# A spectral mixing layer and its MLP: GpSimd's groups and the filter copy moved forward in the first batch, the second batch's evacuations shared by two engines

## The chip, the cores and the metric

One core of a Trainium2 chip runs the whole kernel. The metric is device time in microseconds (us), from launch to end. "Span" is a little less: the time from the first to the last instruction in a profiled execution. Runs of one kernel differ here by about 2 us. Times are therefore compared over several runs, and traces stage by stage. All runs below are fast ones. Engines: ACT is ScalarE, DVE is VectorE.

## The reference

```python
# x (8, 3008, 256), filt_r and filt_i (1505, 256), all fp32
X = np.fft.rfft(x, axis=1)
y = np.fft.irfft(X * (filt_r + 1j * filt_i)[None], n=3008, axis=1)
h = y.reshape(24064, 256) @ w_in            # w_in (256, 2048)
out = np.maximum(0.01 * h, h) @ w_out       # w_out (2048, 256)
```

## The kernel before

The transform of 3008 points is split as 94 x 32. Per batch: matmuls over 94 (`s1`), evacuation (a copy out of PSUM, where matmuls leave their results) to fp16, 32x32 transposes on DVE (`t1`), matmuls over 32 (`s2`), the filter product, matmuls back (`sa`), evacuation, transposes (`t2`), matmuls (`sb`). The MLP runs in slots of one hidden-layer group each; the transform of the next batch is interleaved into these slots. The first batch has nothing to hide behind, so it has code of its own, in two halves of 128 channels, where some filter products go to DVE straight from PSUM, and some to GpSimd by way of a copy by ACT.

```python
outp = ctx.enter_context(tc.tile_pool(name="outst", bufs=4))
php = ctx.enter_context(tc.tile_pool(name="php", bufs=2, space=bass.MemoryType.PSUM))
pfp = ctx.enter_context(tc.tile_pool(name="pfp", bufs=3, space=bass.MemoryType.PSUM))
...
def s1_group(b, g):                      # two matmuls into one PSUM buffer, one evacuation
    def go():
        ps = pfp.tile([P, 2, D], FP32, tag="pf", ...)
        ...
        spread(big[(4 * b) % 3], 2 * g, ps, nc.scalar.copy)      # L174
    return go
...
def first_s2(hf, c, n, on_pool):
    ps = php.tile([P, n, DH], FP32, tag="ph", ...)
    for j in range(0, n, 4):
        nc.tensor.matmul(...)                                     # L253
    if on_pool:
        y = [outp.tile([P, n, DH], FP16, tag="ost", ...) for i in range(2)]
        for j, xf in enumerate(xs):
            act(xf[:], ps[:, ts(j, 4), :])                        # L261
        ... nc.gpsimd.tensor_tensor(y[i]..., AL.mult)             # L264
    else:
        y = [ypp.tile([P, n, DH], FP16, tag=f"yw{i}", bufs=2, ...) for i in range(2)]
        for i in range(2):
            nc.vector.tensor_tensor(y[i][:], ps[:], fs[i], AL.mult)   # L269
def first_sa(hf, c): ...                 # reads y (L277), evacuated by ACT (L174)
def upper(hf): ...                       # filter copied to partitions 64-127: fa by ACT, fb by DVE (L282)
...
plan(1, 0, 0, 3, 6, 10, 4, 3, 25, 31)    # batch 1: s1 from slot 0, three a slot; t1 at 6, s2 at 10, t2 at 25, sb at 31
for slot in range(SL * (NCHUNK + 1)):
    ci, g = divmod(slot, SL)
    if ci < NCHUNK: moe1_group(ci, g)    # 4 matmuls (L339), leaky ReLU by ACT (L344)
    for f in tasks.get(slot, ()): f()
    if ci > 0: moe2_slice(ci - 1, g)     # 8 matmuls (L353)
```

Cuts are marked by dots. `t1` is L186, `t2` L194, the later batches' `s1` L163, `s2` L203, `sb` L230.

Of the kernel before, what the change touches and what calls it, by code (L numbers as in the profile page):

```python
# [65 lines left out]
def kernel(  # L66
# [9 lines left out]
    nc = tc.nc  # L76
# [25 lines left out]
    big = [cpool.tile([P, Q * D], FP16, name=f"big{i}") for i in range(3)]  # L102
# [19 lines left out]
    def x_load(b, n0=0, nn=N2, d0=0, dn=D):  # L122

        for lo, cnt in ((0, R1),) if b + 1 < B else ((0, 64), (64, N1 - 64)):
            nc.gpsimd.dma_start(  # L125
                x_sb[lo : lo + cnt, ds(n0, nn), ds(d0, dn)],
                bass.AP(tensor=x.tensor, offset=x.offset + (b * N + lo * N2 + n0) * D + d0,
                        ap=[[N2 * D, cnt], [D, nn], [1, dn]]))
# [10 lines left out]
    step = N2 // FP  # L139
# [15 lines left out]
    nc.vector.memset(big[2][:].rearrange("p (e n t) -> p e n t", n=Q, t=2)[:, :, NC:Q, :], 0.0)  # L155


    def s1_group(b, g):
        def go():
            ps = pfp.tile([P, 2, D], FP32, tag="pf", name=f"s1_b{b}_g{g}")  # L160
            for j in range(2):
                n2 = 2 * g + j
                nc.tensor.matmul(ps[:, j, :], f1_sb[:N1, n2, :], x_sb[:N1, n2, :],  # L163
                                 start=True, stop=True)
            spread(big[(4 * b) % 3], 2 * g, ps, nc.scalar.copy)
        return go


    def paired(t):
        return t[:].rearrange("p (e n t) -> p n e t", n=Q, t=2)  # L170

    def spread(dst, n0, ps, copy, e0=0):
        nn, de = ps.shape[1], ps.shape[2] // 2
        copy(paired(dst)[:, ds(n0, nn), ds(e0, de)], ps[:].rearrange("p n (e t) -> p n e t", t=2))  # L174
# [3 lines left out]
    def t1_part(b, i, flat=False):  # L178
        def go():
            a = big[(4 * b) % 3][:].bitcast(FP32)[:, ts(i, E4 * Q)].rearrange("p (e n) -> p e n", n=Q)  # L180
            o = big[(4 * b + 1) % 3][:].bitcast(FP32)
            if flat:
                o = o[:, ts(i, E4 * Q)].rearrange("p (e n) -> p e n", n=Q)
            else:
                o = o.rearrange("p (n e) -> p e n", n=Q)[:, ts(i, E4), :]
            nc.vector.transpose(o, a)  # L186
        return go


    def t2_part(b, i):  # L190
        def go():
            a = big[(4 * b + 2) % 3][:].bitcast(FP32)[:, ts(i, E4 * Q)].rearrange("p (e n) -> p e n", n=Q)
            o = big[(4 * b + 3) % 3][:].bitcast(FP32).rearrange("p (h n e) -> p h e n", h=2, n=Q)
            nc.vector.transpose(o[:, i // 2, ts(i % 2, E4), :], a)  # L194
        return go
# [3 lines left out]
    def s2_group(b, g):  # L199
        def go():  # L200
            ps = pfp.tile([P, 2, D], FP32, tag="pf", name=f"s2_b{b}_g{g}")
            src = big[(4 * b + 1) % 3][:].rearrange("p (n d) -> p n d", n=Q)
            nc.tensor.matmul(ps[:], fwd2, src[:, ds(2 * g, 2), :], start=True, stop=True)  # L203
            fa, fb = fa_sb[:, ds(2 * g, 2), :], fb_sb[:, ds(2 * g, 2), :]
            p1 = scrp.tile([P, 2, D], FP32, tag="p1", name=f"p1_b{b}_g{g}")
            p2 = scrp.tile([P, 2, D], FP32, tag="p2", name=f"p2_b{b}_g{g}")
            nc.vector.tensor_tensor(p1[:], ps[:], fa, AL.mult)  # L207
            nc.vector.tensor_tensor(p2[0:64], ps[64:P], fb[64:P], AL.mult)  # L208
            nc.vector.tensor_tensor(p2[64:P], ps[0:64], fb[0:64], AL.mult)  # L209
            y1 = ypp.tile([P, 2, D], FP16, tag="y", name=f"y_b{b}_g{g}")  # L210
            nc.gpsimd.tensor_tensor(y1[:], p1[:], p2[:], AL.add)  # L211
            ys[(b, g)] = y1
        return go

    def sa_group(b, g):
        def go():
            ps = pfp.tile([P, 2, D], FP32, tag="pf", name=f"sa_b{b}_g{g}")
            nc.tensor.matmul(ps[:], inv2, ys.pop((b, g))[:], start=True, stop=True)  # L218
            spread(big[(4 * b + 2) % 3], 2 * g, ps, nc.scalar.copy)
        return go  # L220

    def sb_group(b, g, copy, pool=(pfp, "pf")):
        dt, h = g // 8, g % 8

        def go():
            src = big[(4 * b + 3) % 3][:].rearrange("p (h n d) -> p h n d", h=2, n=Q)
            ps = pool[0].tile([P, 4, N1], FP32, tag=pool[1], name=f"sb_b{b}_g{g}")
            for j in range(4):
                n2 = 4 * h + j
                nc.tensor.matmul(ps[:, j, :], src[:, dt, n2, :], i1_sb[:, n2, :],  # L230
                                 start=True, stop=True)
            yv = yts[b % 2][:, dt, :].rearrange("p (a c) -> p a c", c=N2)
            copy(yv[:, :, ds(4 * h, 4)], ps[:].rearrange("p c a -> p a c"))  # L233
        return go
# [3 lines left out]
    act, dve = nc.scalar.copy, nc.vector.tensor_copy  # L238
# [10 lines left out]
    def first_s2(hf, c, n, on_pool):  # L249
        ps = php.tile([P, n, DH], FP32, tag="ph", name=f"f2_h{hf}_c{c}")  # L250
        src = paired(big[1])
        for j in range(0, n, 4):
            nc.tensor.matmul(ps[:, ds(j, 4), :].rearrange("p n (e t) -> p n e t", t=2), fwd2,  # L253
                             src[:, ds(c + j, 4), ts(hf, DH // 2)], start=True, stop=True)
        fs = [f[:, ds(c, n), ts(hf, DH)] for f in (fa_sb, fb_sb)]
        if on_pool:
            y = [outp.tile([P, n, DH], FP16, tag="ost", name=f"fy{i}_h{hf}_c{c}") for i in range(2)]
            xs = [scrp.tile([P, 4, DH], FP32, tag=f"p{j // 4 + 1}", name=f"fx_h{hf}_c{c + j}")
                  for j in range(0, n, 4)]
# [4 lines that stand above are left out]
                    nc.gpsimd.tensor_tensor(y[i][:, ts(j, 4), :], xf[:], fs[i][:, ts(j, 4), :], AL.mult)  # L264
        else:
            y = [ypp.tile([P, n, DH], FP16, tag=f"yw{i}", bufs=2, name=f"fy{i}_h{hf}_c{c}")
                 for i in range(2)]
            for i in range(2):
                nc.vector.tensor_tensor(y[i][:], ps[:], fs[i], AL.mult)  # L269
        ys[(hf, c)] = y  # L270

    def first_sa(hf, c):
        y = ys.pop((hf, c))
        for j in range(0, y[0].shape[1], 4):
            ps = pfp.tile([P, 4, DH], FP32, tag="pf", name=f"fa_h{hf}_c{c + j}")
            for i, m in enumerate((inv2, inv2x)):
                nc.tensor.matmul(ps[:], m, y[i][:, ds(j, 4), :], start=(i == 0), stop=(i == 1))  # L277
            spread(big[2], c + j, ps, act, hf * DH // 2)

    def upper(hf):  # L280
        for t, cp in ((fa_sb, act), (fb_sb, dve)):
            cp(t[64:P, :, ts(hf, DH)], t[0:64, :, ts(hf, DH)])  # L282
# [9 lines left out]
        first_s1(0, g, two[(g // 2) % 2], (act, dve)[g % 2])  # L292
    t1_part(0, 0, True)(), t1_part(0, 1, True)()
    upper(0)
    first_s2(0, 0, 8, False)
    first_s2(0, 8, 8, True)
    first_s2(0, 16, 4, False)
    first_s2(0, 20, 4, True)
    for g in range(8):
        first_s1(1, g, two[0], dve if g in (1, 3, 6) else act)  # L300
    x_load(1)
    t1_part(0, 2, True)(), t1_part(0, 3, True)()
    first_sa(0, 0), first_sa(0, 16)
    upper(1)
    first_s2(1, 0, 8, False)
    first_s2(1, 8, 8, True)
    nc.gpsimd.dma_start(w_out_sb[:], moe_w_out.rearrange("(ct p) d -> p ct d", p=P))
    first_sa(0, 8), first_sa(0, 20)
    first_s2(1, 16, 8, False)
    first_sa(1, 0)  # L310
    t2_part(0, 0)(), t2_part(0, 1)()
    first_sa(1, 16), first_sa(1, 8)
# [57 lines left out]
    def at(slot, f):  # L370
        tasks.setdefault(slot, []).append(f)

    def plan(b, s1, first, per, t1, s2, step, lag, t2, sb):
        for i, g in enumerate(range(first, 16)):
            at(s1 + i // per, s1_group(b, g))
        if b + 1 < B:
            at(s1 + (15 - first) // per, lambda: x_load(b + 1))
        for i in range(4):
            at(t1 + i, t1_part(b, i))
            at(t2 + i, t2_part(b, i))  # L380
        for g in range(12):
            at(s2 + (step * g) // 4, s2_group(b, g))
            at(s2 + lag + (step * g) // 4, sa_group(b, g))
        for g in range(16):
            at(sb + g // 2, sb_group(b, g, nc.vector.tensor_copy))

    plan(1, 0, 0, 3, 6, 10, 4, 3, 25, 31)
    for b in range(2, B):
        z = 47 * (b - 1) - 8
        plan(b, z, 0, 2, z + 9, z + 13, 5, 3, z + 32, z + 37)  # L390

    for slot in range(SL * (NCHUNK + 1)):
        ci, g = divmod(slot, SL)
# [36 lines left out]
```

## Time and profile before

| | before |
|---|---|
| time, 6 runs | median 793.71 us, 792.79 to 795.1 |
| profiled execution | 792.51 us, span 790.6 us |
| first batch: 17th matmul of `s1` to first MLP matmul | 11.59 to 44.73 = 33.14 us |
| first to ninth MLP group | 44.73 to 60.44 = 15.71 us |
| ninth MLP group to end | 730.20 us |

The lower three rows are differences of start times in the trace. The first stage is counted from the 17th matmul because that one waits for the input's second transfer, whose landing differs from run to run. The prediction shows the profile's lines and reads them.

### The profile page before, as it was taken

Reading aid. Unit: us, or ns where it says so; the run is one execution under the profiler, and the core shown is the slowest. Engines: PE = TensorE matmul, PEld = TensorE weight load, DVE = VectorE, ACT = ScalarE, POOL = GpSimd, SP = SyncE. Lnnn points to the kernel's source line nnn. Section 1 sums busy time; section 2 is a strip of 40 time slices with the busy share of each in tenths; the row PEclk is TensorE's granted clock in tenths of the full one; section 3 lists DMA queues with packets and bytes.
Section 4 is the critical chain, followed back from the end, with each engine's and each line's share of the span. In section 5 each row is a group of like instructions: output and inputs, shape, how many; then the busy total and the mean of one; then the engine's idle time right before and its main releaser. Section 6 shows DMA issues by size and latency. Waiting matters only on the chain.

```text
span 790.6 us, 13456 instructions
## 1 busy us (share of the span) xinstructions
PE 761.7 (96%) x5748; PEld 526.2 (67%) x5748; DVE 362.5 (46%) x451; ACT 560.3 (71%) x802; POOL 150.6 (19%) x122
## 2 busy tenths in 40 slices
PE   2788999999999999999999999999999999999998
PEld 1345667666776667866678667776677666776666
DVE  4829751675407742376415763077431765200000
ACT  3696768777596766877677776877759776666664
POOL 5863400151002500043000420024000340000000
PEclk9999999999999999999999999999999999999999
DMA  9933101410114010410105010141100101001111
GB/s 175 220 44 86 40 28 41 108 41 27 42 41 107 28 41 28 94 54 34 35 29 119 27 41 34 35 106 41 41 27 28 41 27 41 35 34 41 41 41 54
DMA packets 42011, 43.38 MB, mean 55 GB/s; under 512 B 14274, under 2 KB 40514, under 8 KB 41282
## 3 DMA queue, kind: packets, MB, share of 16 engines
q0 software_dynamic: 15760, 16.99, 13.2%
q1 hardware_dynamic: 26192, 25.53, 9.3%
q8 instruction: 45, 0.74, 0.4%
q14 instruction: 14, 0.11, 0.0%
HBM read 34.10 MB, written 24.64 MB: 74 GB/s over the span
## 4 chain that ended last, share of the span: by engine, by line
PE 92%; ACT 3%; DVE 3%; DMA 1%; issue 0%; POOL 0%; ACTq 0%; DVEq 0%; POOLq 0%
PE po_ps L353 40%; PE h_c_g L339 40%; PE sb_b_g L230 3%; PE s_b_g L163 3%; PE s_b_g L203 2%; PE sa_b_g L218 2%; ACT big L174 2%; DVE big L186 1%; DMA x_sb<-in_x_dram 1%; DVE big L194 1%; PE o_c_t L353 1%; ACT gt_c L344 1%; DVE fy_h_c L269 1%; PE f_h_g L244 1%; PE f_h_c L253 1%
## 5 line engine op out<-in xcount | busy, mean ns | idle before, releaser
L344 ACT ACTIVATE gt_c<-h_c_g 128x1024 f16<-128x1024 f32 x376 | 385.6, 1026 | 196.3 <-PE h_c_g L339 195.3
L339 PE MATMUL h_c_g<-yt,w_in_sb 128*128 128x512 f16 (+7 forms) x1728 | 386.7, 351 | 1.3 <-ACT gt_c L344 1.0
L353 PE MATMUL po_ps<-w_out_sb,gt_c 128*128 128x256 f16 x2944 | 381.4, 272 | 0.5 <-ACT ost_c_t L360 0.5
L353 PEld LDWEIGHTS <-gt_c 128*128 128x128 f16 x3008 | 290.7, 98 | 88.7 <-issue 3.8
L339 PEld LDWEIGHTS <-w_in_sb 128*128 128x128 f16 x1728 | 163.0, 98 | 96.2 <-issue 2.3
L211 POOL TENSOR_TENSOR y_b_g<-p_b_g,p_b_g 128x512 f16<-128x512 f32 x84 | 106.9, 1273 | 225.0 <-DVE p_b_g L209 225.0
L186 DVE STREAM_TRANSPOSE big<-big 128x1024 f32<-128x1024 f32 x32 | 55.7, 1844 | 141.6 <-ACT big L174 141.5
L233 DVE CAST yt<-sb_b_g 128x376 f16<-128x376 f32 x116 | 58.3, 545 | 89.9 <-PE sb_b_g L230 89.9
L207 DVE TENSOR_TENSOR p_b_g<-s_b_g,fa_sb 128x512 f32<-128x512 f32 x84 | 58.1, 692 | 37.3 <-PE s_b_g L203 34.8
L360 ACT COPY ost_c_t<-po_ps 128x256 f32<-128x256 f32 x184 | 69.4, 377 | 7.1 <-PE po_ps L353 5.9
L194 DVE STREAM_TRANSPOSE big<-big 128x1024 f32<-128x1024 f32 x32 | 58.4, 1940 | 34.2 <-ACT big L174 34.2
L174 ACT CAST big<-s_b_g 128x512 f16<-128x512 f32 x112 | 61.5, 621 | 0.0
L208 DVE TENSOR_TENSOR p_b_g<-s_b_g,fb_sb 64x512 f32<-64x512 f32 x84 | 58.2, 693 | 1.1
L125 POOL DMA_DIRECT2D x_sb<-in_x_dram x12 | 8.5, 713 | 263.0 <-PE s_b_g L163 262.2
L209 DVE TENSOR_TENSOR p_b_g<-s_b_g,fb_sb 64x512 f32<-64x512 f32 x84 | 57.4, 684 | 1.1
L174 ACT CAST big<-sa_b_g 128x512 f16<-128x512 f32 x84 | 50.6, 602 | 0.0
L230 PEld LDWEIGHTS <-big 128*128 128x128 f16 x512 | 28.7, 98 | 16.6 <-DVE big L194 2.5
L163 PE MATMUL s_b_g<-x_sb,f_sb 94*128 94x256 f16 x224 | 34.6, 272 | 1.6 <-ACT big L174 0.7
L230 PE MATMUL sb_b_g<-i_sb,big 128*128 128x94 f16 x512 | 32.5, 206 | 2.0 <-DVE big L194 1.5
L203 PE MATMUL s_b_g<-big,small_sb 128*128 128x512 f16 x84 | 31.8, 379 | 1.8 <-DVE big L186 1.8
L218 PE MATMUL sa_b_g<-y_b_g,small_sb 128*128 128x512 f16 x84 | 31.8, 379 | 0.0
L163 PEld LDWEIGHTS <-f_sb 94*128 94x128 f16 x224 | 20.9, 97 | 12.2 <-issue 4.4
(37 smaller groups left out, 135.5 us busy)
## 6 DMA issues: line engine op xcount, KB each, us to landing
out_dram<-ost_c_t SPq DMA_DIRECT2D x92, 256.0 KB, 2.1
x_sb<-in_x_dram POOLq DMA_DIRECT2D x6, 1536.0 KB, 10.8
x_sb<-in_x_dram POOLq DMA_DIRECT2D x4, 384.0 KB, 10.4
w_in_sb<-in_moe_w_in_dram POOLq DMA_DIRECT2D x1, 1024.0 KB, 15.3
w_out_sb<-in_moe_w_out_dram POOLq DMA_DIRECT2D x1, 1024.0 KB, 10.7
x_sb<-in_x_dram POOLq DMA_DIRECT2D x1, 1024.0 KB, 8.0
f_sb<-fwd_const SPq DMA_DIRECT2D x4, 192.0 KB, 3.5
fa_sb<-in_filt_r_dram POOLq DMA_DIRECT2D x4, 192.0 KB, 10.0
```

The source lines that it names most:

```text
L163: nc.tensor.matmul(ps[:, j, :], f1_sb[:N1, n2, :], x_sb[:N1, n2, :], start=True, stop=True)
L174: copy(paired(dst)[:, ds(n0, nn), ds(e0, de)], ps[:].rearrange("p n (e t) -> p n e t", t=2))
L186: nc.vector.transpose(o, a)
L194: nc.vector.transpose(o[:, i // 2, ts(i % 2, E4), :], a)
L208: nc.vector.tensor_tensor(p2[0:64], ps[64:P], fb[64:P], AL.mult)
L211: nc.gpsimd.tensor_tensor(y1[:], p1[:], p2[:], AL.add)
L230: nc.tensor.matmul(ps[:, j, :], src[:, dt, n2, :], i1_sb[:, n2, :], start=True, stop=True)
L233: copy(yv[:, :, ds(4 * h, 4)], ps[:].rearrange("p c a -> p a c"))
L339: nc.tensor.matmul(ph[:, j, ds(o, ln)], w_in_sb[:, dt, ts(ct, P)], yts[b % 2][:, dt, ds(lo, ln)], start=(dt == 0), stop=(dt == NDT - 1),)
L344: nc.scalar.activation(gts[ci][:, ds(2 * g, 2), :], ph[:], AF.Lrelu)
L353: nc.tensor.matmul(po, gts[ci][:, ct, ts(tj, P)], w_out_sb[:, ct, :], start=(ct == 0), stop=(ct == NCT - 1))
L360: nc.scalar.copy(ost[:, tj % 2, :], po)
```

## The change

Intent: bring the slower GpSimd products of the first batch forward, and take ACT's long filter copy (2.75 us) off the way of DVE; in the second batch, let the idle DVE take half of the evacuations that ACT is late with, and put the step that follows two slots later, when its data are there.

```diff
-    def s1_group(b, g):
+    def s1_group(b, g, copy=nc.scalar.copy):
...
-            spread(big[(4 * b) % 3], 2 * g, ps, nc.scalar.copy)
+            spread(big[(4 * b) % 3], 2 * g, ps, copy)
...
     upper(0)
+    first_s2(0, 8, 8, True)
     first_s2(0, 0, 8, False)
-    first_s2(0, 8, 8, True)
+    first_s2(0, 20, 4, True)
     first_s2(0, 16, 4, False)
-    first_s2(0, 20, 4, True)
...
+    upper(1)
     first_sa(0, 0), first_sa(0, 16)
-    upper(1)
-    first_s2(1, 0, 8, False)
     first_s2(1, 8, 8, True)
...
+    first_s2(1, 0, 8, False)
+    first_s2(1, 16, 8, False)
     first_sa(0, 8), first_sa(0, 20)
-    first_s2(1, 16, 8, False)
...
-            at(s1 + i // per, s1_group(b, g))
+            at(s1 + g // per, s1_group(b, g, dve if b == 1 and g % 2 else act))
...
-    plan(1, 0, 0, 3, 6, 10, 4, 3, 25, 31)
+    plan(1, 0, 3, 6, 12, 4, 3, 26, 31)
```

Left out are lines that rename things or reorder the plan. One of these matters: the loop that queues the second transposes now stands behind the one of the filter steps, because in the second batch the last `sa` and the first of these transposes now meet in slot 26. For the later batches the order of instructions stays the same.

More of the change, by code (lines that the diff above doesn't have):

```diff
@@ L371, in at, with plan @@
         tasks.setdefault(slot, []).append(f)
-    def plan(b, s1, first, per, t1, s2, step, lag, t2, sb):
-        for i, g in enumerate(range(first, 16)):
-            at(s1 + i // per, s1_group(b, g))
+    def plan(b, s1, per, t1, s2, step, lag, t2, sb):
+        for g in range(16):
+            at(s1 + g // per, s1_group(b, g, dve if b == 1 and g % 2 else act))
         if b + 1 < B:
-            at(s1 + (15 - first) // per, lambda: x_load(b + 1))
+            at(s1 + 15 // per, lambda: x_load(b + 1))
         for i in range(4):
             at(t1 + i, t1_part(b, i))
-            at(t2 + i, t2_part(b, i))
         for g in range(12):
@@ L383, in plan @@
             at(s2 + lag + (step * g) // 4, sa_group(b, g))
+        for i in range(4):
+            at(t2 + i, t2_part(b, i))
         for g in range(16):
-            at(sb + g // 2, sb_group(b, g, nc.vector.tensor_copy))
-    plan(1, 0, 0, 3, 6, 10, 4, 3, 25, 31)
+            at(sb + g // 2, sb_group(b, g, dve))
+    plan(1, 0, 3, 6, 12, 4, 3, 26, 31)
     for b in range(2, B):
         z = 47 * (b - 1) - 8
-        plan(b, z, 0, 2, z + 9, z + 13, 5, 3, z + 32, z + 37)
+        plan(b, z, 2, z + 9, z + 13, 5, 3, z + 32, z + 37)
     for slot in range(SL * (NCHUNK + 1)):
```

## The prediction

> **What bounds the kernel now.** I read the page's table of engines first, then busy times by stage, then the chain of waits through the first 67 us, then timelines of single engines there.
>
> ```profile
> PE 761.7 (96%) x5748; PEld 526.2 (67%) x5748; DVE 362.5 (46%) x451; ACT 560.3 (71%) x802; POOL 150.6 (19%) x122
> ```
>
> TensorE is busy for 761.7 of 790.6 us, so at most 28.9 us can be had from reordering. The table by stage says where they lie (start:end, length, busy us and instructions of PE, PEld, DVE, ACT, POOL, then the granted clock, DMA share and GB/s):
>
> ```profile
> 16.80:24.35 7.55, 6.27 (x38) 3.70 (x39) 6.59 (x8) 3.89 (x8) 5.31 (x6) 1.00 1.70 221
> 24.35:35.30 10.95, 6.92 (x24) 2.18 (x24) 8.35 (x9) 8.57 (x12) 7.58 (x8) 1.00 1.06 230
> 35.30:44.70 9.40, 7.21 (x79) 4.38 (x79) 8.79 (x8) 6.97 (x16) 9.32 (x2) 1.00 1.02 146
> 44.70:59.00 14.30, 11.95 (x60) 5.78 (x60) 0.40 (x1) 13.01 (x22) 7.46 (x2) 1.00 0.01 2
> 59.00:66.80 7.80, 5.54 (x33) 3.15 (x33) 7.23 (x4) 5.65 (x7) 0.00 (x0) 1.00 1.03 200
> 66.80:760.00 693.20, 692.65 (x5279) 483.65 (x5279) 324.88 (x416) 500.25 (x710) 110.08 (x90) 1.00 0.16 46
> ```
>
> From 66.8 us on TensorE is full: 692.65 of 693.2. Work there is only carried forward, so the time saved is the amount by which TensorE reaches that full state earlier, for the same work done. Before it lie two stretches that the change touches: the first batch (to 44.7) and the slots in which the second batch's first transform runs between the first MLP groups (44.7 to 66.8). The chain of waits (start, length, what) for the second:
>
> ```profile
> 46.91 1.58 ACT big L174 x3
> 48.50 0.92 ACT gt_c L344
> 49.41 1.47 ACT big L174 x3
> 50.88 0.93 ACT gt_c L344
> ...
> 58.98 0.49 ACT big L174
> 59.47 0.02 issue
> 59.49 7.24 DVE big L186 x4
> 66.73 0.04 issue
> 66.78 0.38 PE s_b_g L203
> ```
>
> ACT alone sets these slots: one leaky ReLU (0.92) and three evacuations (0.49 each), 2.39 us a slot. Then four DVE transposes follow end to end, and the PE timeline shows TensorE standing still for them:
>
> ```profile
> 63.91 1.03 PE L339 MATMUL h_c_g<-yt,w_in_sb 128*128 128x512 f16 x4
> 66.78 0.38 PE L203 MATMUL s_b_g<-big,small_sb 128*128 128x512 f16 x1 [1.84 <-DVE big L186]
> ```
>
> The same chain in the first batch, where the filter copy (L282) is on the path:
>
> ```profile
> 26.62 2.76 ACT fa_sb L282
> 29.38 0.02 issue
> 29.41 2.37 DVE fy_h_c L269 x2
> 31.77 0.05 issue
> 31.82 1.04 PE f_h_c L253 x2
> 32.85 0.02 issue
> 32.88 2.36 DVE fy_h_c L269 x2
> 35.23 7.28 DVE big L194 x4
> ```
>
> [...] the same evacuation shape (128x512 to f16) takes 0.69 us on DVE and 0.60 on ACT in the first batch. [...] GpSimd runs one 15.74 us negation from 35.82 to 51.56, over the moved evacuations. [...] DVE's casts out of PSUM at 43.11 to 45.09, under that negation, take 540 to 550 ns, and 545 is the mean of all 116. [...] here 128-column matmuls are 0.107 us apart up to about 23 us and 0.054 soon after.
>
> **The change, part by part.**
>
> (a) Slots 0 to 5: eight of 16 evacuations go from ACT to DVE, which is idle there (14.40 us before its transposes). ACT loses 8 x 0.48 = 3.85 us. ACT per pair of slots: 2 x 0.92 + 3 x 0.48 = 3.28; TensorE per pair: two MLP groups of 0.865 and six transform steps of 0.215 = 3.02; DVE 3 x 0.69 = 2.07. So ACT stays the bound, narrowly, at 1.64 a slot, and the queue of three PSUM buffers adds small waits. I stepped through the slots with the program's own buffer order (in the built program, group 3 reuses the buffer of 1, 4 of 0, 5 of 2, 6 of 3, 7 of 5, ...), intervals from the trace, 0.38 us from a step's issue to its end, 0.69 for DVE. MLP group 8 then issues at 56.50 where the trace of before has 60.44: 3.94 us gained.
>
> (b) The transposes start when the last evacuation ends: about 55.1 instead of 59.49, so they end at 62.35. The transform that needs them is also moved, from slot 10 to 12. From group 8 on a slot takes 0.865 + 0.87 = 1.735 us, so slot 12 starts at 56.50 + 4 x 1.735 = 63.44 and its first filter matmul would issue at 64.30, two us after the transposes. The wait disappears: from the issue end of the last MLP matmul (63.91 + 4 x 0.217 = 64.78) to 66.78 that is 2.00 us (the 1.84 of the timeline counts a modelled end). As TensorE has no gap later, moving the matmuls to a later slot costs nothing by itself.
>
> (c) Second transposes one slot later (26), their users still from slot 31. Before, the first starts 2.67 us after slot 24 begins (97.86 less 95.19) and four take 7.30. After: slot 26 + 2.67 + 7.30 = + 9.97; the first user is at + 9.75 (0.865 + 0.215 + 0.87 + 4 x 1.735 + 0.865) but needs only the first two transposes, done at about + 6.4. No stall.
>
> (d) First batch, first half. GpSimd's groups now come first through TensorE, so DVE's first filter product waits for the fourth matmul: 18.73 instead of 17.96. Its two products then end at 21.08, not 20.31. In the built program groups 20 and 16 now share one PSUM buffer, so 16 also waits for ACT's copy of 20: matmul at 20.24, ready at 20.83, hidden behind DVE. DVE reaches the next evacuation at 22.37 instead of 21.84, + 0.5. TensorE's group 4 waits for that buffer and group 7 in turn for group 4's, so the transposes start at about 25.4 instead of 24.92.
>
> (e) First batch, second half. The filter copy starts when ACT's last evacuation is done, 25.4, ends at 28.15 instead of 29.37, and leaves the path. But DVE's group is now second in TensorE: transposes end 27.29 + 0.49 = 27.78, the fourth matmul 1.93 later, so the product starts at about 29.75 against 29.41. Had (d) cost nothing, (e) would have gained only 0.15. From there the same steps follow (2.37, 1.09, 2.36, transposes): + 0.34 us at the start of the MLP. The evacuations pushed behind the copy end at about 35.2, just before the transposes need them at 35.5.
>
> Sum: - 3.94 - 2.00 + 0.34 = - 5.6 us. Nothing else moves: later batches have the same instructions in the same order.
>
> **The rivals.**
> 1. The reordering of the first batch pays as intended: the 1.13 us that DVE waits for the filter copy goes. For it: that wait is on the chain. Against: the copy's removal exposes TensorE's fourth matmul 0.15 us later. Time 786.3.
> 2. Buffers bind rather than ACT in slots 0 to 5: for it, three PSUM buffers and TensorE at 3.02 per 3.28; a chain matmul, evacuation, matmul costs about 1.1 us a group. If half of (a) is lost, 789.8.
> 3. The moved evacuations are slowed by GpSimd's negation. Only those before 51.56 can be, about four; doubled, that costs up to 2 us: 789.8. The 540 to 550 ns above speak against it.
> 4. The compressed distance between second transposes and their users stalls TensorE at slot 31. Were the dependency on all four transposes, 9.97 against 9.75 plus latency would cost some 0.3 us.
> 5. The gain is hidden, since TensorE is 96% busy: 793. Against it: the chain of waits has the slots' ACT work and the transposes on it, and TensorE never waits later for anything that could absorb them.
>
> **Range and chances.** 793.4 - 5.6 = 787.8 us. The first batch is uncertain by about a microsecond either way ([...]tight buffers), the slots by about 0.7, and the three runs of before spread over 2.3. Range 786.0 to 789.6. A change of 2% would be 15.9 us, more than half of all idle time of TensorE and three times my sum; nothing lengthens the full stretch. Faster by over 2%: 0.01; within: 0.98; slower: 0.01.
>
> **What would show it.** (a) ACT's leaky ReLUs in slots 0 to 5 come alternately about 1.9 and 1.4 us apart; eight DVE casts of 128x512 at about 0.69 us. (b) No wait of the filter matmul (L203) for the transposes (L186). (c) No wait of L230 for L194 after 100 us. (d), (e) The DVE product L269 of the second half waits for TensorE, not for the copy L282, and starts near 29.75; the first MLP matmul at about 45.1. Full state at the second batch's first filter matmul: about 64.6. The prediction is wrong if the MLP starts before 44.5 or after 45.8, if a slot still takes over 1.9 us on average, or if TensorE's idle time does not fall by about 5 to 6 us.

## The result, and the profile after

The changed kernel took 788.21 us (median of 6 runs, 787.49 to 789.27), before in the same rounds and earlier 793.71. The ratio is 0.9931, interval 0.9918 to 0.9944. The output is correct. Predicted were 787.8 us and a range from 786.0 to 789.6.

The page's engine line of the changed kernel: TensorE has the same 5748 matmuls, in a span that is 3.9 us shorter.

```profile
PE 762.2 (97%) x5748; PEld 527.3 (67%) x5748; DVE 367.9 (47%) x459; ACT 557.1 (71%) x794; POOL 150.6 (19%) x122
```

The stages of the changed kernel, with the same columns as in the prediction (stretch, length, busy us and instructions of PE, PEld, DVE, ACT, POOL, then clock, DMA share, GB/s):

```profile
25.00:36.00 11.00, 8.02 (x21) 2.47 (x20) 8.41 (x8) 7.18 (x10) 2.03 (x3) 0.84 1.08 237
46.60:58.46 11.86, 11.12 (x64) 6.18 (x64) 7.23 (x10) 10.57 (x15) 10.51 (x2) 1.00 0.27 37
58.46:66.30 7.84, 7.84 (x53) 5.08 (x52) 6.00 (x4) 5.55 (x7) 0.00 (x0) 1.00 0.82 173
66.30:756.00 689.70, 689.15 (x5256) 481.34 (x5255) 324.71 (x416) 499.18 (x708) 110.07 (x90) 1.00 0.16 46
```

The slots that took 14.30 us for 11.95 us of TensorE's work now leave it 0.74 us idle in 11.86, and from 58.46 on TensorE is full; before it was from 66.8. The first line is a warning: the mean clock is 0.84 there, and GpSimd worked only 2.03 us in that stretch, against 7.58 in the one of before. (The clock column counts the time before the first record of the clock as full. Here that record comes at 28.56 us, and the L277 matmuls before it are 0.43 us apart, as they are from 33.4 to 35.1 us, where the record says half, against 0.22 from 35.4 us on, so the clock was at half there. The spacing of L253's matmuls does not tell: in the kernel before they are 0.41 to 0.43 us apart both from 16.82 us, ahead of the clock's rise at 23.3, and from 27.34, behind it, and no run shows why.)

The chain of waits of the changed kernel through the slots (start, length, what): leaky ReLUs still follow ACT's evacuations, but now with two and one of these in turn, and the filter matmul L203 follows an MLP matmul, not the transposes.

```profile
48.80 1.12 ACT big L174 x2
49.92 0.90 ACT gt_c L344
50.82 0.52 ACT big L174
51.34 0.94 ACT gt_c L344
...
65.61 0.86 PE h_c_g L339 x4
66.47 0.22 PE s_b_g L203
```

The same chain in the first batch:

```profile
30.14 2.37 DVE fy_h_c L269 x2
...
33.62 2.37 DVE fy_h_c L269 x2
...
36.13 3.40 POOL fy_h_c L264 x3
...
39.57 0.39 PE fa_h_c L277
...
39.98 0.60 ACT big L174
...
40.61 3.79 DVE big L194 x2
```

The filter copy is no longer just ahead of DVE's product, as intended. The view names ACT's evacuations there instead, which end last before the product starts. What the product needs is the fourth matmul: it starts 0.71 us after that matmul's issue, as it starts 0.70 us after the second one's in copy_only below. And GpSimd's products are now on the chain: the last two transposes wait for them. The third starts 28.80 us into the stage, against 27.16 before, which is nearly all that the stage lost. The timeline of GpSimd, first in the kernel before, then in the changed one:

```profile
30.07 2.27 POOL L264 TENSOR_TENSOR fy_h_c<-fx_h_c,fa_sb 128x512 f16<-128x512 f32 x2 [3.37 <-ACT fx_h_c L261]
```

```profile
35.01 2.28 POOL L264 TENSOR_TENSOR fy_h_c<-fx_h_c,fa_sb 128x512 f16<-128x512 f32 x2 [8.97 <-issue]
```

Its inputs, ACT's two copies, were both ready at 31.06 us, and yet it started at 35.01. The bracket names no releaser; the program does: this product writes into one of four buffers of the pool, the one that held the first half's product, and waits until TensorE has read that. The reading matmuls now stand behind the group of columns 16 to 23, which waits for DVE.

Stage by stage (start times in the traces):

| stage | before | after | change | predicted |
|---|---|---|---|---|
| 17th `s1` matmul to first MLP matmul | 33.14 | 34.81 | + 1.67 | + 0.34 |
| first to ninth MLP group | 15.71 | 11.89 | - 3.82 | - 3.94 |
| ninth MLP group to end | 730.20 | 728.21 | - 1.99 | - 2.00 |

The sum is - 4.1 us in this pair of traces, where the times say - 5.5. So the two lower rows came as predicted, the upper one did not, and one pair of traces isn't typical. The clock has a part in it. The stages of the changed kernel cut where the granted clock changes:

```profile
28.56:31.97 3.41, 1.48 (x4) 0.23 (x2) 2.37 (x3) 2.50 (x5) 0.00 (x0) 1.00 1.21 250
31.97:35.39 3.41, 2.84 (x7) 1.01 (x8) 2.28 (x3) 0.66 (x2) 0.38 (x1) 0.50 0.99 211
```

After a stretch in which TensorE was busy for only 1.48 us, and in which a wait of 2.50 us for DVE began, its clock was half for 3.41 us, just when the first half's products were to be read. In the trace of before the clock was up from 23.3 us and stayed up to the end of the work; here it came up only at 28.56.

### The profile page after: what moved, and what is told of

It is laid out like the page before. It is cut to its first block, busy times and chain, and to the rows that moved or that the text cites. A ratio compares the mean times of both kernels' runs of the same rounds, so it can differ in the third digit from the quotient of the medians. Undisturbed runs are those within 1.5% of the kernel's fastest.

```text
span 786.7 us, 13456 instructions
## 1 busy us (share of the span) xinstructions
PE 762.2 (97%) x5748; PEld 527.3 (67%) x5748; DVE 367.9 (47%) x459; ACT 557.1 (71%) x794; POOL 150.6 (19%) x122
## 4 chain that ended last, share of the span: by engine, by line
PE 93%; ACT 3%; DVE 2%; DMA 1%; POOL 1%; issue 1%; POOLq 0%; ACTq 0%; DVEq 0%
PE po_ps L353 41%; PE h_c_g L339 40%; PE sb_b_g L230 3%; PE s_b_g L163 3%; PE s_b_g L203 2%; PE sa_b_g L218 2%; DMA x_sb<-in_x_dram 1%; ACT big L174 1%; DVE fy_h_c L269 1%; PE o_c_t L353 1%; ACT gt_c L344 1%; DVE big L194 0%; PE f_h_g L244 0%; POOL fy_h_c L264 0%; ACT fa_sb L282 0%
## 5 line engine op out<-in xcount | busy, mean ns | idle before, releaser
L207 DVE TENSOR_TENSOR p_b_g<-s_b_g,fa_sb 128x512 f32<-128x512 f32 x84 | 58.1, 692 | 38.8 <-PE s_b_g L203 35.9
L194 DVE STREAM_TRANSPOSE big<-big 128x1024 f32<-128x1024 f32 x32 | 58.6, 1935 | 35.2 <-ACT big L174 35.2
L174 ACT CAST big<-s_b_g 128x512 f16<-128x512 f32 x104 | 56.9, 606 | 0.0
L230 PEld LDWEIGHTS <-big 128*128 128x128 f16 x512 | 28.8, 98 | 15.4 <-DVE big L194 1.1
L230 PE MATMUL sb_b_g<-i_sb,big 128*128 128x94 f16 x512 | 32.5, 206 | 1.1 <-DVE big L194 0.6
L203 PE MATMUL s_b_g<-big,small_sb 128*128 128x512 f16 x84 | 31.8, 379 | 0.0
```

The source lines that it names most:

```text
L174: copy(paired(dst)[:, ds(n0, nn), ds(e0, de)], ps[:].rearrange("p n (e t) -> p n e t", t=2))
L194: nc.vector.transpose(o[:, i // 2, ts(i % 2, E4), :], a)
L207: nc.vector.tensor_tensor(p1[:], ps[:], fa, AL.mult)
L230: nc.tensor.matmul(ps[:, j, :], src[:, dt, n2, :], i1_sb[:, n2, :], start=True, stop=True)
```

## The experiments

Theory A: the slots give the whole gain; the first batch's new order costs time, because GpSimd waits for its buffers. Rivals: B, the first batch's order pays and the slots give less; C, the clock alone made the first batch longer; D to H as named below. Eleven kernels ran, all with correct results, each over five rounds against the kernel before on the same chip. "Stage" is the first batch's, as in the table above.

### slots_only: the first batch as before

```diff
 # the changed kernel, with the first batch's calls in the order of before
-    first_s2(0, 8, 8, True)
     first_s2(0, 0, 8, False)
+    first_s2(0, 8, 8, True)
 ... (and so on: all lines of the first batch)
```

> The changed kernel with the first batch put back into the old order; the slots share their evacuations and the second batch's filter step stays at slot 12. Theory A (the slots give all of the gain, 3.9 us from ACT and 2.0 us from the transposes; the new order of the first batch costs time): 5.9 us faster than before, so 0.4 to 1.9 us faster than the changed kernel; in the trace 11.8 us from the first MLP matmul to the ninth MLP group and no wait of the filter matmul L203. Rival B (the new order of the first batch pays, and the slots give less than 5.5): it comes out slower than the changed kernel, by 0.5 us or more.

Measured: 786.92 us (before 792.97), ratio 0.9923 (0.9911 to 0.9936), or - 6.1 us. In the trace 11.94 us from the first to the ninth MLP group, 728.23 to the end, no wait of L203. The slots give all of the gain. Rival B falls: this is not slower than the changed kernel. The old order's stage took 33.99 us in this trace, not 33.14, and the clock fell to half from 32.5 to 35.9 us. The same order took 33.85 us in s2_slot10 and 35.07 in two_thirds below: the trace of before that the prediction worked from is the shortest of four.

### first_only: only the first batch changed

```diff
 # the kernel before, with the first batch's calls in the new order
+    first_s2(0, 8, 8, True)
     first_s2(0, 0, 8, False)
-    first_s2(0, 8, 8, True)
 ... (and so on: all lines of the first batch)
```

> The kernel before with only the first batch in the new order. Theory A: 0.4 to 1.9 us slower than before, with GpSimd's second-half products starting at about 35 us instead of 30, after TensorE has read the first-half ones, and the chain of waits going through them. Rival B: faster than before by about 0.5 to 1.1 us, since the filter copy leaves the chain.

Measured: 793.37 us against 792.97, ratio 1.0009 (0.9996 to 1.0021). The interval just includes no difference; the mean is 0.7 us worse. GpSimd's second-half products started at 33.72 us, 23.2 us into the stage, exactly as far as in the changed kernel, and not at the 35 us of absolute time that I wrote, because the input landed 1.3 us earlier. L264 was not on this trace's chain (the reading matmuls and ACT's evacuations were, with the clock at half from 29.9 to 36.7 us), so this part of the expectation missed. The stage was 34.81 us, as in the changed kernel. No gain of 0.5 to 1.1 us: rival B falls again.

### reads_first: the reads of GpSimd's products back in front

```diff
-    first_s2(1, 16, 8, False)
     first_sa(0, 8), first_sa(0, 20)
+    first_s2(1, 16, 8, False)
```

> The changed kernel, with the second half's group of columns 16 to 23 put back behind the matmuls that read GpSimd's first-half products; all else as in the changed kernel. Theory A (GpSimd waits for the buffers of these products, which only those matmuls free, and that is what the first batch lost): GpSimd's second-half products start at about 31 us, L264 leaves the chain of waits, the first MLP matmul comes about 1 to 1.5 us earlier than in a run of the changed kernel, time 787.0 to 787.8. Rival C (what was lost in the changed kernel's trace was the TensorE clock, which went back to half between 32.0 and 35.4 us, not the buffers): the same time as the changed kernel within 0.3 us.

Measured: 786.62 us, ratio 0.9926 (0.9912 to 0.994). GpSimd started at 29.75 us, L264 left the chain, stage 33.65: 1.16 us shorter than in the changed kernel, and the clock did not fall. The marks in the trace agree with A; the time is 0.4 us below the 787.0 to 787.8 that A named. It is level with slots_only (0.9923), but the interval overlaps that of the changed kernel too, so it is the trace, not the time, that shows what the one line carried: 1.16 us of the stage. It does not settle A against C, since the clock stayed up too.

### s2_slot10: the filter step left at slot 10

```diff
 # slots_only, and
-    plan(1, 0, 3, 6, 12, 4, 3, 26, 31)
+    plan(1, 0, 3, 6, 10, 4, 3, 25, 31)
```

> As slots_only, but the filter step stays at slot 10 and the second transposes at slot 25. Theory A: the transposes end 7.3 us after the last evacuation, at 64.5 us by the changed kernel's trace, and the filter matmul at slot 10 would be ready at 62.8: a wait of about 1.6 us, so 1.6 us slower than slots_only. Rival D (the move to slot 12 is not needed once the evacuations are shared): within 0.3 us of slots_only.

Measured: 789.38 us, ratio 0.9952 (0.9939 to 0.9965), 2.5 us slower than slots_only. The wait of TensorE is back in the timeline:

```profile
64.54 0.38 PE L203 MATMUL s_b_g<-big,small_sb 128*128 128x512 f16 x1 [1.43 <-DVE big L186]
```

By start times it is 64.54 less the 62.95 at which the matmul would have followed (ninth group at 58.62, two slots of 1.735 and a group of 0.865): 1.6 us, as expected, and the ninth group to the end takes 729.79 instead of 728.2. The rest of the 2.5 us is not shown: in this trace the input landed 2 us later than in slots_only's, and the intervals are about 1 us wide to either side. Rival D falls: sharing the evacuations alone would have left a good quarter of the gain on the table, and moving the step costs nothing in the trace.

### copy_only: the filter copy ahead, DVE's groups still first

```diff
 # slots_only, and
+    upper(1)
     first_sa(0, 0), first_sa(0, 16)
-    upper(1)
```

> slots_only with one line of the first batch moved: the second half's filter copy ahead of the three evacuations, while DVE's groups stay first through TensorE. First-batch stage (from the 17th matmul of the first transform to the first MLP matmul) in traces so far: 33.1 to 34.0 us in the old order, 34.8 in the new, 33.65 in reads_first. Theory A (the copy pays if DVE's group comes first, because then its product waits for neither the copy nor the fourth matmul; GpSimd's groups going first eat that): the second half's first DVE product starts about 17.0 us into the stage instead of 18.6, stage 32.2 to 32.7, about 1.3 us less time than slots_only. Rival E (the copy is hidden anyway, the next wait takes its place): same as slots_only within 0.4 us.

Measured: 786.19 us, ratio 0.9904 (0.9889 to 0.992), stage 32.41: 0.7 us below slots_only by median, against 1.3 expected; by the ratios it is 1.5 us. The two ran in different rounds, so I take 0.7 to 1.5. Its chain of waits:

```profile
25.40 2.75 ACT fa_sb L282
...
28.95 2.37 DVE fy_h_c L269 x2
...
34.77 7.28 DVE big L194 x4
```

The product starts at 28.95, 17.1 us into the stage (17.0 expected; 18.6 in slots_only), and the four transposes run without a wait. Rival E falls by the trace; by time alone it would not, as the intervals overlap. So the two parts of the first batch's change pull against each other: the copy's move pays, and putting GpSimd's groups first takes it away, because DVE's group is then third and fourth among the four matmuls. Compare reads_first, which has the copy ahead, no buffer wait, and the clock up from 25.7 us: its product starts 18.33 us into the stage and its stage is 33.65, each about 1.2 us later than here.

### more_bufs and warm_gap: take away the buffer wait, or the slow clock

```diff
 # more_bufs: the changed kernel, and
-    outp = ctx.enter_context(tc.tile_pool(name="outst", bufs=4))
+    outp = ctx.enter_context(tc.tile_pool(name="outst", bufs=6))
 # warm_gap: the changed kernel, and filler matmuls, overwritten later
+    keep_warm(6)
     first_s2(1, 16, 8, False)
```

> The changed kernel with six buffers instead of four in the pool that GpSimd's products come from, so that the second half's products need not wait until the first half's are read. Theory A (buffers): GpSimd's second-half products start within 0.2 us of the end of ACT's copies, about 19.3 us into the first-batch stage instead of 23.2; stage 34.8 down to about 34.1 or less; DVE's third second transpose no longer waits for the chain through L264; 0.5 to 1 us faster than the changed kernel. Rival C (the clock): stage stays at 34.6 to 34.9 if the clock is at half again around 30 to 36 us.

> The changed kernel with six filler matmuls of 512 columns in TensorE's 2.5 us gap before the group of columns 16 to 23; their output is overwritten later. They keep TensorE's clock up and remove no wait. Theory A (buffers, made worse by a slow clock): the reads of the first-half products run at full rate, GpSimd starts about 22.3 us into the stage instead of 23.2, stage about 33.9 to 34.1. Rival C (the clock is all of it): stage down to 33.5, the predicted one. If the clock falls anyway, 34.8 again.

Measured: more_bufs 787.38 us, ratio 0.9929 (0.9916 to 0.9942), stage 34.66. GpSimd started at 31.01, 18.8 us into the stage, and was off the chain, so the buffers were what it waited for:

```profile
31.01 2.26 POOL L264 TENSOR_TENSOR fy_h_c<-fx_h_c,fa_sb 128x512 f16<-128x512 f32 x2 [4.59 <-ACT fx_h_c L261]
```

(The MLP's outputs are staged in the same pool, so the edit is not one of the first batch alone; the stage ends before the first of them.) But the stage was hardly shorter: in this trace the clock was half from 33.5 to 36.9 us, and the reads that stand late then took 2.58 us for six matmuls; ACT's evacuations behind them held the transposes. That is what C said. warm_gap: 787.19 us, ratio 0.9925 (0.9913 to 0.9938), stage 34.17, the clock up from 25.9 us without a fall. GpSimd started 22.6 us into the stage (22.3 expected), and the third transpose still waited for it:

```profile
33.37 2.29 POOL L264 TENSOR_TENSOR fy_h_c<-fx_h_c,fa_sb 128x512 f16<-128x512 f32 x2 [8.32 <-issue]
```

Neither A alone nor C alone holds: each cost stands behind the other.

### bufs_and_warm: both

```diff
 # the changed kernel, with both edits of the pair above
```

> The changed kernel with both: six buffers for GpSimd's products and six filler matmuls in TensorE's gap. Each alone moved the first-batch stage little (34.81 to 34.66 and 34.17). Theory G (two costs lie side by side, the buffer wait and the slow clock, and each hides the other): with both gone and the clock up in the trace, the stage is the predicted 33.3 to 33.6 us, and the third second transpose follows the second without a wait. Rival H (a third cost in the new order): 34.0 or more although the clock is up.

Measured: 787.15 us, ratio 0.9921 (0.9908 to 0.9933), stage 33.77 with the clock up from 27.3 us. Its chain goes from DVE's product to the four transposes in one go:

```profile
32.27 2.36 DVE fy_h_c L269 x2
34.62 7.38 DVE big L194 x4
```

So G holds as to the waits: 1.04 us of the stage go when both are gone. The stage itself is 0.2 us above the expected window and below H's, so a small remainder isn't named. In time the pair gains 0.8 us by the ratios and 1.1 by the medians, within the intervals.

### two_thirds: more evacuations on DVE

```diff
 # slots_only, and
-            ... s1_group(b, g, dve if b == 1 and g % 2 else act))
+            ... s1_group(b, g, dve if b == 1 and g % 3 else act))
```

> slots_only with two of three evacuations of the second batch's first transform on DVE instead of one of two. By the trace's durations ACT would need 0.92 + 0.48 = 1.40 us a slot and TensorE 1.51, DVE 1.3 to 1.4. If ACT is what sets the slots (theory): the stretch from the first MLP matmul to the ninth MLP group goes from 11.9 to about 11.3 us, now set by TensorE, 0.5 us less time than slots_only. Rival F (buffers: each group waits for DVE's evacuation, 0.69 us, rather than ACT's): 11.9 or more.

Measured: 785.9 us, ratio 0.991 (0.9894 to 0.9926), 11.32 us from the first to the ninth MLP group (11.94 in slots_only). Leaky ReLUs of its ACT timeline are now 1.54 us apart, all alike, where the changed kernel has 1.9 and 1.47 in turn:

```profile
51.26 1.02 ACT L344 ACTIVATE gt_c<-h_c_g 128x1024 f16<-128x1024 f32 x1
52.18 0.61 ACT L174 CAST big<-s_b_g 128x512 f16<-128x512 f32 x1
52.80 1.02 ACT L344 ACTIVATE gt_c<-h_c_g 128x1024 f16<-128x1024 f32 x1
```

ACT did set the slots; three PSUM buffers are enough. Rival F falls. That TensorE sets them now, as expected, is not clear: the chain runs through TensorE in the first three slots and through ACT from 51.26 us on, so the two are about even. By time it is 1.0 us below slots_only, in other rounds, where 0.5 was expected. Its first batch is that of slots_only, and took 35.07 us with the clock at half from 35.1 to 41.9 us: another draw of the clock, and the old order at its worst is as long as the new one.

### copy_two_thirds and copy_warm: a version that beats both

```diff
 # copy_two_thirds: slots_only with the edits of copy_only and of two_thirds
 # copy_warm: copy_two_thirds, and fillers of 94x512 behind the first half's first transform
+    early_warm(7)
     t1_part(0, 0, True)(), t1_part(0, 1, True)()
```

> Both gains together: copy_only's first batch and two of three evacuations on DVE. If they add: first-batch stage 32.4 us where the clock is up, 11.3 us to the ninth MLP group; time 0.6 us below copy_only, about 0.9 us below two_thirds, near 785.2. If they don't add (the clock or a buffer takes the difference): level with copy_only.

> copy_two_thirds with seven filler matmuls in the 3.4 us in which TensorE waits for the first transposes of the first batch; their output is overwritten. If the clock is what makes runs of one kernel differ: the clock is up within about 8 us of the stage's start instead of 12 to 16, the second part of the first transform runs at full rate, stage 31.5 to 32.2, 0.3 to 0.8 us less than copy_two_thirds, with less spread. If the fillers delay the filter matmuls behind them, up to 0.3 us slower.

Measured: copy_two_thirds 784.8 us (784.35 to 785.26, 4 runs), ratio 0.989 (0.9875 to 0.9905), stage 32.40 and 11.43 us to the ninth group. In the trace both gains add: it is 8.8 us faster than before and by the medians some 3.4 us faster than the changed kernel, though in other rounds. This is the version to keep. copy_warm: 785.04 us, ratio 0.9896 (0.9883 to 0.991), stage 32.42. The fillers filled the gap (TensorE waited 0.37 us instead of 3.36), but the clock rose no sooner, at 27.2 us, 16.4 into the stage, although TensorE was busy for 6.72 of the 8 us up to 16.0 and for all of the 7.1 from 19.1 to 26.2. So the expectation that filling the gap brings the rise forward fell here; why it rose so late stays open.

## Why the prediction was right, and where not

The time came out close: 787.8 against 788.21, and a gain of 5.6 against 5.5 us. By its own steps:

- (a) right. 3.94 predicted, 3.82 measured; ACT still set the slots, with spacings of 1.9 and 1.47 us in turn, and DVE's casts at 0.69 us. s2_slot10 and two_thirds have the same stretch at 11.89 and, with less on ACT, 11.32. Rival 2 (buffers) did not show. Nor did rival 3: GpSimd's 15.74 us negation lay over seven of the eight casts (it ended at 56.51, the last cast began at 56.36), and they took 0.69 us each, as did the seven of this shape in the first batch of the kernel before, all ahead of its negation (they began by 23.91 us, it at 35.82).
- (b) right. 2.00 against 1.99. Taking the move back costs 1.6 us in the stage (s2_slot10).
- (c) right. No wait of L230 for L194 behind 100 us. The first user came at 104.49 us and the last transpose ended at 104.60, 0.11 us apart where 0.22 was worked out.
- (d) right. The second half's transposes began 13.9 us into the stage (25.74 less 11.81); predicted were 13.8 (25.4 less 11.59).
- (e) right up to DVE's product: predicted 18.2 us into the stage, measured 18.3. The step that failed is the sentence behind it, "From there the same steps follow". They don't: the reordering put the reads of GpSimd's first-half products behind a group that waits for DVE, and with four buffers GpSimd's second-half products had to wait for these reads. The prediction follows the PSUM buffers and does not mention this pool. With the clock up, the buffer wait still left the stage at 34.17 (warm_gap); with the clock down and no buffer wait it was 34.66 (more_bufs); with neither 33.77 (bufs_and_warm), 0.3 above the 33.48 that the sum implied. The trace showed + 1.67 instead of + 0.34.
- The MLP started at 46.6 us, outside the 44.5 to 45.8 that I had named as the mark of a wrong prediction. TensorE's idle time fell from 28.9 to 24.5 us, by 4.4 and not by the 5 to 6 that was the third mark. The part on the first batch was wrong by these marks, even though the time came out close.

Why did the total fit all the same? In part by luck. Parts (a) and (b) make up 5.94 of the predicted sum and came out at 5.81. The missed term is the small one, and over the runs the new order cost less than in the pair of traces: + 0.7 us by first_only's times, with an interval from - 0.3 to + 1.7. The traces agree with that when all are used: the stage averages 34.0 us in the four with the old order (33.14 to 35.07), and it is 34.81 in both with the new order unmodified, + 0.8. The pair shows + 1.67 because its trace of before is the shortest of the four: the clock was up 12 us into the stage and did not fall. So the mis-sized term, + 0.34, is 0.4 to 0.5 too small, and the range of 786.0 to 789.6 was wide enough to hide it.

The clock's part in this is not fully separated. It fell in all three traces that keep the new order and have no fillers (the changed kernel, first_only, more_bufs), in two of the four with the old order (slots_only and two_thirds), and in neither with fillers in the gap (warm_gap, bufs_and_warm). Perhaps the new order's longer gap (TensorE waits 2.5 us for DVE ahead of L253 in the changed kernel and first_only, 1.3 us before, 1.8 in s2_slot10, 1.9 in slots_only) makes the fall likelier, but that is not shown: slots_only and s2_slot10 have the same first batch, and the clock fell in slots_only alone.

Rival 1 (the reordering pays) was wrong for the whole, and right for one part: copy_only shows that the copy's move pays if DVE's groups stay first.

## What to carry to other kernels

Where one engine is full from some point on, count a change as the amount by which that point comes earlier for the same work done, stage by stage; the two stages worked out that way here came within 0.12 us. Before moving a group of instructions ahead of others, look for every buffer that the instructions now standing behind would have freed, in SBUF pools as well as in PSUM. And take a single trace of a short, thinly filled stage as one draw: input landing (10.46 to 12.87 us) and clock (the same order took 33.14 us without a fall of the clock and 35.07 with one) moved the start by more than the effect in question (0.8).
